# Two of the seven products of a large block as three passes over 12-bit parts

## The chip, the cores and the metric

The kernel runs on one core of a Trainium2 chip. The metric is the device time of one execution in microseconds (us), lower is better. The core has a matrix engine (TensorE, PE in the profile, with PEld for its weight loads), a vector engine (VectorE, DVE), a scalar engine (ScalarE, ACT), a general engine (GpSimd, POOL), and a queue that issues DMA transfers (SyncE, SP). Each engine carries out its own instructions strictly in order; semaphores make one wait for another. All data here are float32.

## The reference

A retention recurrence over 4 batches, 8 heads, 768 positions and 64 channels gives 3072 tokens of 512 channels; behind it stands a two-layer network with an ELU. What is computed:

```python
state = gamma[None, :, None, None] * state + np.einsum('bhd,bhe->bhde', k[:, :, t], v[:, :, t])
y[:, :, t] = scale * np.einsum('bhd,bhde->bhe', q[:, :, t], state)
...
x = attn_out.transpose(0, 2, 1, 3).reshape(B * S, H * D)
h = x @ w_in                                          # (3072, 512) @ (512, 2048)
g = np.where(h > 0.0, h, np.exp(np.minimum(h, 0.0)) - 1.0)
return (g @ w_out).astype(np.float32)                 # (3072, 2048) @ (2048, 512)
```

## The kernel before

The retention runs in chunks of 128 positions; four chunks make a block of 512 tokens, six blocks in all. Its steps (`retention_step`, `scores`, `states`) are spread among the matrix products of the network. `load` fetches a chunk (1024 KB), `scale_v` (L293) multiplies its values, on GpSimd mostly.

Both products of the network use the Strassen-Winograd scheme: a product of matrices cut in 2x2 quarters is made of seven products M1 to M7 of sums of quarters in place of eight. In this kernel's numbering the sums of the first GEMM's result are

- C11 = M1+M2
- C21 = M1+M6+M7+M4
- C22 = M1+M6+M7+M5
- C12 = M1+M6+M5+M3

Block 0 has a plain first GEMM. Block 1 uses the scheme once, in four columns n = 0 to 3 (`first(n)`, L732, and `strassen`, L730 and before it). In a column the products P1, P2, P6, P7, P5, P3, P4 follow each other on TensorE at 1.73 us each, and between them the loop over n (L1567 on) interleaves the end of the column before, the decoding of weights, sums of weights for later blocks, and retention steps. The column's copies (`kept`, L714) lift a product off PSUM on ScalarE; P6 of a column continues on the bank that P1 used, so it waits for that copy.

Blocks 2 and 3, and 4 and 5, form two large blocks of 1024 tokens (nb = 0 and 1). Their first GEMM uses the scheme with large quarters. M2, M3, M1 and M7 are themselves computed by an inner Strassen-Winograd, `big_twice`, in eight steps `at` = 0 to 7 (two per product). The results are kept in SBUF: M2 and M3 in the places of C11 and C12, M7 in that of C22, M1 in a tile of its own. Beside these steps VectorE works off `xparts`, the sums of inputs that the products need; `big_layer_x` makes those of M7, M5, M6 and M4. Then M6, M4 and M5 follow as plain products, in a loop over eight tiles n of 128 rows by 512 columns (L1676 to L1815 and `big_rest`, L1194). A large weight slice of 256 KB per product and pair of tiles is kept in a ring of slots; `want` names the slices in order, `done` gives a slot back and issues the next fetch on SP.

In that loop, per tile: a seed copies M1 into a PSUM bank (L1657), M6 is added there by two matmuls, a second seed (L1661) copies this sum to a second bank, M4 is added there and M5 to the first. VectorE adds M7, or M7 and M3, or the sum for C12, from SBUF (`big_sum`, L1211). The ELU of each result is begun on ScalarE by a Relu and an Exp (`big_elu`, L1217 and L1218, three buffers r) and ended on VectorE (L1219). The engine orders are those in which the program issues: the schedule is made by hand.

After the loop `second_big` (L1236 on) makes the second GEMM of the large block, again with an inner scheme; its products (L1251), copies `ms` (L1259) and sums run over 128x256 tiles. Its first input sums (L1233 and L897) lie at the end of the loop. SBUF is cut into pools: `mpool` holds lifted products and results, `stage` and `t4` serve the early part, and the ring `wq` and the input sums `ts` use their space later. PSUM has banks a (2), b, d, f, and four shared ones (`ps_r`).

Lines of the code before that the steps touch: L293 (`scale_v`), L501 and L502 (ELU of block 1), L714, L719 (copies and sums of `strassen`), L768 (its products), L1155, L1166 and L1170 (products, lifts and sums of `big_twice`), L1202, L1211, L1217 to L1219, L1233, L1251, L1259.

Of the kernel before, what the change touches and what calls it, by code (L numbers as in the profile page):

```python
# [10 lines left out]
FP32 = mybir.dt.float32  # L11
I32 = mybir.dt.int32
# [3 lines left out]
ALU = mybir.AluOpType  # L16


@with_exitstack
def kernel(  # L20
# [7 lines left out]
    scratch4: bass.AP,  # L28
    out: bass.AP,
# [55 lines left out]

    early = ctx.enter_context(ExitStack())
    stage = early.enter_context(tc.tile_pool(name="stage", bufs=3, side="right"))
    t4 = early.enter_context(tc.tile_pool(name="t4", bufs=1, side="right"))
# [792 lines left out]
    PLANE = {6: 0, 5: 1, 4: 2}  # L881

    def send_layer(j, ns):

        for n in ns:
            to_send.append((
                scratch4[PLANE[j], n].rearrange("p (f c) -> p f c", f=2), LAYER[j][:, n].rearrange("p f k c -> p f (k c)")
            ))

    xs = {}  # L890
# [176 lines left out]
    ts_slots = []  # L1067

    def next_ts():
        ts_slots.append(ts_slots.pop(0))  # L1070
        return ts_slots[-1]
# [4 lines left out]
    def want_first(n):  # L1076
# [7 lines left out]
        def layer(j, m):  # L1084
            if n:
                want((tb, "r", j, m), scratch4[PLANE[j], m])

# [11 lines left out]
        for m in range(NQ):  # L1099
            layer(6, m)  # L1100
            if m == 0:
                piece(*before, 3)
            layer(4, m)
            layer(5, m)
# [3 lines left out]
    def big_x(j):  # L1108

        x, t, first_k = xb2 if j == 3 else xa, next_ts(), 0 if j == 1 else 2  # L1110
        yield from inner_x(j, t, *(x[:, first_k + k, TH * u : TH * u + TH] for k in range(2) for u in range(2)))
# [9 lines left out]
    def big_layer_x():  # L1121

        sub = lambda o, x, y: nc.vector.tensor_tensor(out=o, in0=x, in1=y, op=ALU.subtract)
        b11, b12, b21, b22 = (
            x[:, 2 * r : 2 * r + 2].rearrange("p k (h t) -> p k h t", h=2) for r in range(2) for x in (xa, xb2)
        )
        t3 = next_ts()
        sub(t3, b22, b12)
        yield
        t1, t2, t7, t4_ = (next_ts() for _ in range(4))  # L1130
        yield from inner_x(7, t7, *(t3[:, a, b] for a in range(2) for b in range(2)))
        layer_x.update({5: t1, 6: t2, 4: t4_})
        sub(t1, b12, b11)
        yield
        sub(t2, b22, t1)
        yield
        sub(t4_, b21, t2)
        yield

    PLACE = {1: "M1", 2: "C11", 3: "C12", 7: "C22"}  # L1140

    def big_twice(n, j, at):
# [20 lines left out]
        def lift(ps, o=None):  # L1163
            if o is None:
                o = mpool.tile([P, 2, TH], FP32, name="m", tag="m")
            nc.scalar.copy(o, ps)  # L1166
            return o
# [26 lines left out]
    def big_rest(n, m, j, ps):  # L1194

        name = (n + 2, "r", j, m // 2)
        if n:
            w = where[name].rearrange("p (f k d) -> p f k d", f=2, k=2)[:, m % 2]
        else:
            w = LAYER[j][:, m // 2, m % 2]  # L1200
        for k in range(2):
            nc.tensor.matmul(  # L1202
                ps, lhsT=w[:, k, :], rhs=layer_x[j][:, k], start=False, stop=(k == 1),
                skip_group_check=True,
# [4 lines left out]
    def big_sum(x, m, ps):  # L1209

        nc.vector.tensor_tensor(out=tile_of(x, m), in0=ps, in1=tile_of("C22" if x == "C21" else x, m), op=ALU.add)  # L1211

    def big_elu(x, m):

        g = tile_of(x, m)
        r = epool.tile([P, 512], FP32, name="r", tag="r", bufs=3).rearrange("p (t c) -> p t c", t=2)
        nc.scalar.activation(r, g, AF.Relu, scale=-1.0)  # L1217
        nc.scalar.activation(r, r, AF.Exp, scale=-1.0)  # L1218
        return lambda: nc.vector.scalar_tensor_tensor(g, r, -1.0, g, ALU.add, ALU.max)  # L1219
# [16 lines left out]
    def second_big(nb, behind_last):  # L1236
# [3 lines left out]
        def input_parts(j):  # L1240
            x = INPUT2[j]
            t = [next_ts() for _ in range(4)]
# [24 lines left out]
        def inner(j):  # L1267
            res = mpool.tile([P, 2, 2, TH], FP32, name="res", tag="m")
# [297 lines left out]
    some(smalls[2], 1)  # L1566
    for n in range(NQ):  # L1567
        if n < 3:
            load(2 * CPB + n)
# [26 lines left out]
        if n in (1, 2):  # L1596
            run(smalls[n + 1])
        send_small()
    retention_step(2, 1)

    early.close()
    ring_ = ctx.enter_context(tc.tile_pool(name="ring", bufs=1, side="right")).tile([P, 8, 512], FP32, name="wq")
# [291 lines left out]
```

## Time and profile before

| | us |
|---|---|
| median of 3 runs (lowest, highest) | 620.64 (619.3, 620.83) |
| profiled execution, its own time | 620.36 |
| span of that execution in the trace | 618.6 |
| loop over the tiles, nb=0 | 293.99 to 336.12 |
| loop over the tiles, nb=1 | 487.62 to 529.75 |
| TensorE busy in 293.90 to 336.10 | 42.20 of 42.20 |
| VectorE, ScalarE busy in that stretch | 36.64, 37.41 |
| mean granted TensorE clock | 1.00 |

The span is the time from the first to the last instruction in the trace; the run's own time is 1.76 us longer. A group of the profile names a line, an engine, an operation, the tile written and the tiles read, how often it ran, the time that it kept its engine busy, the mean time of one in ns, and the idle time before it with the instruction or transfer that ended most of it. An instruction that reads `x2` in a timeline stands for a run of two equal ones. A float32 matmul leaves two records in the trace.

### The profile page before, as it was taken

The page shows a single profiled execution, that of the slowest core. Times are in us where ns is not written, and L with a number is a line of the kernel's source. Part 1 is how long each engine was busy: PE and PEld are TensorE (multiplying, and loading weights), DVE is VectorE, ACT ScalarE, POOL GpSimd, SP SyncE. Part 2 cuts the span into 40 slices and gives each one's busy share as a digit, 9 for nine tenths or more (in the row PEclk, how much of TensorE's full clock was granted, in tenths as well). Part 3 has the DMA queues.
Part 4 walks back from the last instruction along what each step waited for, and adds up shares of the span by engine and source line. Part 5 has one row for each costly group of instructions (what it writes and reads, how often), then busy time and mean ns, then how long its engine had stood idle before and what let it go on. Part 6 is the DMA issues. An engine that isn't in the chain of part 4 may idle for free.

```text
span 618.6 us, 13412 instructions
## 1 busy us (share of the span) xinstructions
PE 610.7 (99%) x5446; PEld 481.2 (78%) x5446; DVE 494.7 (80%) x777; ACT 261.0 (42%) x446; POOL 22.1 (4%) x29
## 2 busy tenths in 40 slices
PE   8999999999999999999999999999999999999997
PEld 6764568888889998888445888888888644788886
DVE  5769889989889776776988987898446888888785
ACT  5889735105542112236887210010244798511110
POOL 2011000000000010000100000110000000000000
PEclk9999999999999999999999999999999999999999
DMA  8698579789575897786902445874555423456552
GB/s 299 283 385 304 181 216 268 214 251 285 186 233 174 307 375 287 261 262 173 310 1 84 123 133 153 284 260 132 187 159 147 134 69 102 118 152 183 154 154 108
DMA packets 79277, 125.13 MB, mean 202 GB/s; under 512 B 6128, under 2 KB 46832, under 8 KB 74480
## 3 DMA queue, kind: packets, MB, share of 16 engines
q1 hardware_dynamic: 79216, 124.28, 62.4%
q8 instruction: 43, 0.70, 0.5%
q14 instruction: 18, 0.15, 0.1%
HBM read 94.63 MB, written 29.62 MB: 201 GB/s over the span
## 4 chain that ended last, share of the span: by engine, by line
PE 89%; DMA 5%; DVE 3%; ACT 1%; SPq 1%; issue 1%; DVEq 0%
PE pa L1251 15%; PE pa L1155 9%; PE pd L1251 8%; PE pa L1202 6%; PE pd L1155 4%; PE pd L1202 4%; PE pb L1251 4%; PE pa L545 3%; PE x L635 3%; DMA wq<-scratch_dram 3%; PE pa L768 3%; PE pa L927 3%; PE pb L1155 2%; PE pa L635 2%; PE pb L1202 2%; PE y L415 2%
## 5 line engine op out<-in xcount | busy, mean ns | idle before, releaser
L1259 ACT COPY ms<-pa 128x256 f32<-128x256 f32 x41 | 15.3, 372 | 108.6 <-PE pa L1251 105.5
L1251 PE MATMUL pa<-gC,wq 128*128 128x256 f32 x224 | 53.1, 381 | 0.0
L1251 PEld LDWEIGHTS pa<-gC,wq 128*128 128x128 f32 x224 | 42.2, 190 | 6.8 <-DVE gT L1219 0.5
L1218 ACT ACTIVATE r<-r 128x512 f32<-128x512 f32 x64 | 40.3, 630 | 2.0
L1166 ACT COPY m<-pa 128x512 f32<-128x512 f32 x32 | 18.7, 585 | 47.4 <-PE pa L1155 47.4
L293 POOL TENSOR_TENSOR chunk<-chunk,vf 128x512 f32<-128x512 f32 x15 | 19.0, 1265 | 377.2 <-DMA chunk<-in_qkv_dram 201.2
L1263 DVE TENSOR_TENSOR res<-pd,ms 128x256 f32<-128x256 f32 x26 | 10.9, 421 | 25.0 <-PE pd L1251 14.2
L1155 PE MATMUL pa<-ts,wq 128*128 128x256 f32 x104 | 26.9, 384 | 0.0
L1251 PE MATMUL pa<-ts,wq 128*128 128x256 f32 x112 | 26.8, 382 | 0.0
L1251 PE MATMUL pd<-w_all,wq 128*128 128x256 f32 x112 | 26.6, 380 | 0.1
L171 ACT ACTIVATE w_all<-wraw 128x1024 uint32<-128x1024 uint32 (+1 forms) x19 | 19.1, 1007 | 14.7 <-PE x L635 9.8
L1251 PE MATMUL pd<-ts,wq 128*128 128x256 f32 x104 | 24.7, 380 | 0.1
L1233 DVE TENSOR_TENSOR gC<-w_all,gC 128x1024 f32<-128x1024 f32 x20 | 24.2, 1259 | 0.0
L1251 PEld LDWEIGHTS pd<-w_all,wq 128*128 128x128 f32 x112 | 21.2, 190 | 3.4 <-DVE w_all L897 0.5
L1251 PEld LDWEIGHTS pa<-ts,wq 128*128 128x128 f32 x112 | 21.0, 190 | 2.9
L173 ACT ACTIVATE w_all<-wraw 128x1024 fp8e4<-128x1024 f32 (+1 forms) x19 | 22.6, 1192 | 0.6
L1251 PE MATMUL pa<-w_all,wq 128*128 128x256 f32 x96 | 22.9, 381 | 0.0
L1155 PEld LDWEIGHTS pa<-ts,wq 128*128 128x128 f32 x104 | 19.3, 190 | 4.4 <-ACT m L1166 0.7
L1219 DVE SCALAR_TENSOR_TENSOR w_all<-r,w_all 128x512 f32<-128x512 f32 x32 | 21.9, 684 | 0.7 <-ACT r L1218 0.5
L1251 PEld LDWEIGHTS pd<-ts,wq 128*128 128x128 f32 x104 | 19.7, 190 | 3.2 <-DVE ts L897 0.5
L1202 PE MATMUL pa<-ts,wq 128*128 128x512 f32 x48 | 22.1, 592 | 0.0
L1202 PE MATMUL pa<-gC,w_all 128*128 128x512 f32 x48 | 22.1, 592 | 0.0
(327 smaller groups left out, 1456.7 us busy)
## 6 DMA issues: line engine op xcount, KB each, us to landing
wq<-scratch_dram SPq DMA_DIRECT2D x191, 256.0 KB, 3.3
chunk<-in_qkv_dram SPq DMA_DIRECT2D x22, 1024.0 KB, 7.3
wraw<-in_w_dram SPq DMA_DIRECT2D x15, 1024.0 KB, 6.6
out_dram<-res SPq DMA_DIRECT2D x7, 512.0 KB, 2.9
scratch_dram<-gT SPq DMA_DIRECT2D x12, 256.0 KB, 4.3
wq<-scratch_dram SPq DMA_DIRECT2D x24, 128.0 KB, 2.9
scratch_dram<-w_all SPq DMA_DIRECT2D x12, 256.0 KB, 3.9
scratch_dram<-w_all SPq DMA_DIRECT2D x24, 128.0 KB, 2.8
```

What stands on the lines that cost most here:

```text
L171: nc.scalar.activation(flat, lo, AF.Copy, scale=2.0**-29)
L173: nc.scalar.activation(top, hi.bitcast(FP32), AF.Copy, scale=2.0**-120, saturate=False)
L293: eng.tensor_tensor(out=v, in0=v, in1=vf[:, i].unsqueeze(2).to_broadcast([C, H, D]), op=ALU.mult)
L545: nc.tensor.matmul(hp, lhsT=w[n][:, fi, j // 2, j % 2, :], rhs=xb[:, j, :], start=(j == 0), stop=(j == 3))
L635: nc.tensor.matmul(X[j][:, d, :], lhsT=w[j][:, d * P : d * P + P], rhs=x[j], start=(n == 0 and d == 0), stop=at_end, skip_group_check=True,)
L1155: nc.tensor.matmul(ps[:, f, :], lhsT=w[:, f, :], rhs=big_xs[j][k], start=(begin and f == 0), stop=True, skip_group_check=True,)
L1166: nc.scalar.copy(o, ps)
L1202: nc.tensor.matmul(ps, lhsT=w[:, k, :], rhs=layer_x[j][:, k], start=False, stop=(k == 1), skip_group_check=True,)
L1218: nc.scalar.activation(r, r, AF.Exp, scale=-1.0)
L1219: return lambda: nc.vector.scalar_tensor_tensor(g, r, -1.0, g, ALU.add, ALU.max)
L1233: nc.vector.tensor_tensor(out=quarter(to, r, t), in0=quarter(x, r, t), in1=quarter(y, r, t), op=op)
L1251: nc.tensor.matmul(ps, lhsT=w[:, f, :], rhs=ts[j][k][:, f // 2, f % 2, :], start=(begin and f == 0), stop=(f == 3), skip_group_check=True,)
```

## The change

M6 and M4 of the large blocks are computed with operands cut into parts of 12 bits, a weight w = hi + lo (scaled by 2^-12 in one part) and an input x likewise. The parts are kept as float32r, a matmul type of the same 4 bytes. Each of M6 and M4 is the sum of three products of parts: two passes into a PSUM bank, a VectorE operation (`six_sum`, `four_sum`) that multiplies the bank by 4097 and adds a sum from SBUF, and a third pass with the difference of the parts. M5 stays a float32 product.

- `parts_of_layer(n)` cuts the weights of M6 and M4 in block 1's first GEMM, for columns 0 (ahead of n=1), 1 (end of n=1), 2 (start of n=2) and 3 (end of n=2): two ScalarE, two VectorE and two GpSimd operations of 128x512, and two sends of 768 KB to a new scratch in DRAM. Its tile, "wide", has one buffer. All weights of M6 and M4 are fetched back in 24 slices of 256 KB for each large block; before, nb=0 used them in SBUF and nb=1 fetched 12 slices for three products.
- `split_x` cuts the inputs of M6 and M4 in steps 5 to 7 of the inner products, with one operation each of 128x1024 on ScalarE, GpSimd and VectorE.
- `seeds` forms M3-M7 in C12's place and M1+M7 in C22's place on GpSimd, 16 operations of 128x512 for each large block. The seed copies into PSUM and their twins are gone.
- The sum for M4 is not taken from a second bank: `u3` is a ScalarE copy of the finished M1+M6+M7. M5 is added on M6's bank, which then is C22; C12 is formed from that bank by VectorE (`c12_sum`). The ELUs of C21 and C22 read PSUM.
- In the loop the ends of C22 come two tiles later, those of C12 four; after the loop, what is left of them stands beside the first products of `second_big`.
- Chunks for the next blocks are loaded in steps 5 and 6 and at tiles 2 and 5, and scaled after the loop. The tiles for lifted products fall from 5 to 3, with pools of their own in places.

```diff
+    def stt(o, a, by, b, op):
+        nc.vector.scalar_tensor_tensor(o, a, by, b, ALU.mult, op)
+    def parts_of_layer(n):
+        t = wide.tile([P, 2, 6, TH], F32R, name="wp", tag="wp")
+        for at, j in ((0, 6), (2, 4)):
+            w = LAYER[j][:, n].rearrange("p f k d -> p f (k d)")
+            hi, lo, d = (t[:, :, x] for x in (at, at + 1, 4 + at // 2))
+            nc.scalar.activation(hi, w, AF.Copy, scale=R * CUT)
+            stt(lo, hi, -4096.0, w, ALU.add)
+            nc.gpsimd.tensor_tensor(out=d, in0=lo, in1=hi, op=ALU.subtract)
+        for f in range(2):
+            to_send.append((
+                scratch5[2 * n + f].rearrange("q p c -> p q c"),
+                t[:, f].rearrange("p (q h) c -> p q (h c)", h=2).bitcast(FP32),
+            ))
...
+    def split_x(hi, lo, d, x):
+        yield nc.scalar.activation(hi, x, AF.Copy, scale=CUT)
+        yield nc.gpsimd.tensor_tensor(out=lo, in0=x, in1=hi, op=ALU.subtract)
+        yield stt(d, lo, -4096.0, hi, ALU.add)
...
     def big_layer_x():
         sub = lambda o, x, y: nc.vector.tensor_tensor(out=o, in0=x, in1=y, op=ALU.subtract)
...
+        b11, b12, b21, b22 = (x[:, 2 * r : 2 * r + 2] for r in range(2) for x in (xa, xb2))
+        t3 = slots_e[3]
+        sub(t3.rearrange("p k h t -> p k (h t)"), b22, b12)
+        yield
+        sub(b12, b12, b11)
+        layer_x[5] = b12
+        yield
+        sub(b22, b22, b12)
+        planes.update(open_planes())
+        first_split = split_x(*planes[6], b22)
+        next(first_split)
+        next(first_split)
+        yield
+        yield from inner_x(7, slots_e[0], *(t3[:, a, b] for a in range(2) for b in range(2)))
+        next(first_split)
+        yield
+        sub(b21, b21, b22)
+        second_split = split_x(*planes[4], b21)
+        next(second_split)
+        next(second_split)
+        yield
+        next(second_split)
+        yield
...
+    def passes(n, m, j, third, ps):
+        name = (n + 2, "C" if third else {6: "A", 4: "B"}[j], m)
+        todo = [(planes[j][2], 0 if j == 6 else 256)] if third else [(planes[j][0], 0), (planes[j][1], 256)]
+        for x, at in todo:
+            for k in range(2):
+                c = at + k * P
+                nc.tensor.matmul(
+                    joined(ps), lhsT=where[name][:, c : c + P].bitcast(F32R), rhs=x[:, k],
+                    start=(not third and c == 0), stop=(k == 1), skip_group_check=True,
+                )
+        if not third or j == 4:
+            done(name)
...
         g = tile_of(x, m)
+        h = g if h is None else h
         r = epool.tile([P, 512], FP32, name="r", tag="r", bufs=3).rearrange("p (t c) -> p t c", t=2)
-        nc.scalar.activation(r, g, AF.Relu, scale=-1.0)
+        nc.scalar.activation(r, h, AF.Relu, scale=-1.0)
         nc.scalar.activation(r, r, AF.Exp, scale=-1.0)
-        return lambda: nc.vector.scalar_tensor_tensor(g, r, -1.0, g, ALU.add, ALU.max)
+        return lambda: nc.vector.scalar_tensor_tensor(g, r, -1.0, h, ALU.add, ALU.max)
...
     for n in range(NQ):
+        if n == 1:
+            sums_of.close()
+            wide = wide_of.enter_context(tc.tile_pool(name="wide", bufs=1, side="right", reuse_waits="tile"))
+            parts_of_layer(0)
+            send_small()
+        elif n == 2:
+            parts_of_layer(2)
+            send_small()
...
             run(smalls[n + 1])
+            parts_of_layer(2 * n - 1)
         send_small()
...
-        def rest(m, j):
-            big_rest(nb, m, j, qd[m] if j == 4 else qa[m])
-        def seed(m):
-            qa[m] = bank("aab"[m % 3])
-            nc.scalar.copy(qa[m], tile_of("M1", m))
-        def second_seed(m):
-            qd[m] = bank("d")
-            (nc.vector.tensor_copy if m in (1, 3, 5) else nc.scalar.copy)(qd[m], qa[m])
-        def sum_(x, m):
-            big_sum(x, m, qd[m] if x == "C21" else qa[m])
+        any_bank = lambda: ps_r.tile([P, 2, TH], FP32, name="x", tag="r")
+        def six(m):
+            q6[m] = any_bank() if m % 4 == 3 else bank("aba"[m % 4])
+            passes(nb, m, 6, False, q6[m])
+        def six_sum(m):
+            stt(q6[m], q6[m], 4097.0, tile_of("C22", m), ALU.add)
+        def four(m):
+            q4[m] = any_bank() if m % 2 else bank("d")
+            passes(nb, m, 4, False, q4[m])
+        def four_sum(m):
+            stt(q4[m], q4[m], 4097.0, u3.pop(m), ALU.add)
+        def c12_sum(m):
+            nc.vector.tensor_tensor(out=tile_of("C12", m), in0=q6[m], in1=tile_of("C12", m), op=ALU.add)
+        def seeds(*ms):
+            for m in ms:
+                x, y, z = tile_of("C12", m), tile_of("C22", m), tile_of("M1", m)
+                nc.gpsimd.tensor_tensor(out=x, in0=x, in1=y, op=ALU.subtract)
+                nc.gpsimd.tensor_tensor(out=y, in0=z, in1=y, op=ALU.add)
...
             for m in ms:
-                ends[x, m] = big_elu(x, m)
+                h = {"C21": q4, "C22": q6}.get(x)
+                ends[x, m] = big_elu(x, m, h and h[m])
...
             if at == 7:
-                seed(0)
+                seeds(0, 1)
...
-        rest(0, 6)
+        six(0)
         big_c11(0, 1)
-        second_seed(0)
         end("C11", 4)
         run(tail)
-        seed(1)
+        seeds(2, 3, 4, 5, 6, 7)
+        six_sum(0)
         begin("C11", 2)
         end("C11", 5)
         for n in range(2 * NQ):
-            if n == 0:
-                rest(0, 4)
-                sum_("C21", 0)
+            passes(nb, n, 6, True, q6[n])
+            u3[n] = mpool.tile([P, 2, TH], FP32, name="m", tag="m")
+            nc.scalar.copy(u3[n], q6[n])
+            four(n)
+            four_sum(n)
+            if n:
+                end("C21", n - 1)
+            else:
                 big_c11(1, 1)
+                begin("C11", 3)
+                end("C11", 2)
             if n < LAST:
-                rest(n + 1, 6)
-            if n == LAST - 1 and nb == 0:
-                ts_slots[2:2] = [
-                    w_all[:, 2 * k : 2 * k + 2, 3072:3584].rearrange("p n (f t) -> p n f t", f=2) for k in range(2)
-                ]
+                six(n + 1)
             if n:
-                begin("C12", n - 1)
+                big_rest(nb, n - 1, q6[n - 1])
+            if n < LAST:
+                six_sum(n + 1)
+            if n > 1:
+                end("C22", n - 2)
+            if n > 3:
+                end("C12", n - 4)
             late = {1: 6, 3: 7}.get(n)
             if late:
                 end("C11", late)
-            if n + 2 <= LAST:
-                seed(n + 2)
+            if n == 2:
+                begin("C11", 7)
+            elif n > 2:
+                begin("C12", n - 3)
             if n:
+                c12_sum(n - 1)
                 begin("C22", n - 1)
-                end("C21", n - 1)
-                end("C12", n - 1)
-            else:
-                begin("C11", 3)
-                end("C11", 2)
-            if n:
-                rest(n, 4)
-                sum_("C21", n)
-            if n < LAST:
-                second_seed(n + 1)
-            begin("C21", n)
-            if n:
-                end("C22", n - 1)
             else:
                 end("C11", 3)
-            if n in (0, 2):
-                begin("C11", 6 + n // 2)
-            if more and n in (0, 1, 3, 5):
-                bring(groups[0], (n + 1) // 2)
+            passes(nb, n, 4, True, q4[n])
+            begin("C21", n)
+            if n == 0:
+                begin("C11", 6)
+            if more and n in (2, 5):
+                load(groups[0] * CPB + 2 + n // 5)
             if n == LAST:
                 next(sec)
                 next(sec)
-            rest(n, 5)
-            sum_("C12", n)
-            sum_("C22", n)
...
+        big_rest(nb, LAST, q6[LAST])
+        end("C22", LAST - 1)
+        end("C12", LAST - 3)
+        begin("C12", LAST - 2)
...
+        end("C21", LAST)
+        c12_sum(LAST)
...
+        begin("C22", LAST)
         next(sec)
+        end("C12", LAST - 2)
+        begin("C12", LAST - 1)
+        next(sec)
+        end("C22", LAST)
+        end("C12", LAST - 1)
         begin("C12", LAST)
-        next(sec)
-        begin("C22", LAST)
-        end("C21", LAST)
         end("C12", LAST)
-        end("C22", LAST)
+        if more:
+            for n in range(CPB):
+                scale_v(groups[0] * CPB + n)
```

## The prediction

> **What bounds the kernel now.** I read the page's busy shares and its chain of waits first: they say which engine sets the end.
>
> ```profile
> PE 610.7 (99%) x5446; PEld 481.2 (78%) x5446; DVE 494.7 (80%) x777; ACT 261.0 (42%) x446; POOL 22.1 (4%) x29
> ...
> PE 89%; DMA 5%; DVE 3%; ACT 1%; SPq 1%; issue 1%; DVEq 0%
> ```
>
> TensorE works 610.7 of 618.6 us, so work taken off it can shorten the run by as much, if nobody else becomes late. Next the stretches, one for block 1's first GEMM, where the change puts the new parts, and one for the loop over the row tiles of the first large block (columns: stretch, its length, then busy time of PE, PEld, DVE, ACT, POOL, the granted clock, the DMA share, GB/s).
>
> ```profile
> 153.00:162.00 9.00, 9.00 (x44) 7.92 (x43) 8.63 (x14) 4.64 (x8) 0.00 (x0) 1.00 0.94 343
> ...
> 293.90:336.10 42.20, 42.20 (x102) 18.96 (x101) 36.64 (x56) 37.41 (x65) 4.38 (x4) 1.00 0.42 138
> ```
>
> The averages of 80% and 42% mislead: in the loop VectorE is busy 87% and ScalarE 89% beside a TensorE that never stops, and in block 1 the DMA stands at 0.94. Those are the two places to fear. Then the loop's instructions by shape (count | busy us, mean ns of one), and its timeline (start, length):
>
> ```profile
> L1202 PE MATMUL pa<-gC,w_all 128*128 128x512 f32 x48 | 22.1, 592 | 0.0
> L1211 DVE TENSOR_TENSOR w_all<-pd,w_all 128x512 f32<-128x512 f32 x8 | 5.5, 691 | 3.1 <-PE pd L1202 3.1
> L1657 ACT COPY pa<-chunk 128x512 f32<-128x512 f32 x5 | 2.9, 581 | 0.0
> ...
> 296.86 1.29 DVE L1219 SCALAR_TENSOR_TENSOR gC<-r,gC 128x512 f32<-128x512 f32 x2
> 298.55 0.69 DVE L1211 TENSOR_TENSOR w_all<-pd,w_all 128x512 f32<-128x512 f32 x1 [0.41 <-PE pd L1202]
> 299.62 0.62 ACT L1217 ACTIVATE r<-gC 128x512 f32<-128x512 f32 x1
> 300.27 0.63 ACT L1218 ACTIVATE r<-r 128x512 f32<-128x512 f32 x1
> 300.81 0.61 ACT L1217 ACTIVATE r<-w_all 128x512 f32<-128x512 f32 x1
> ```
>
> So: a float32 product of 128x512 is two records; 49 products fill 42.1 us, 0.86 us each, 0.43 a record. VectorE issues 128x512 operations 0.60 apart when queued (two in 1.29), ScalarE a Relu-Exp pair every 1.19 (299.62 to 300.81: 0.65 and 0.54), a copy takes 0.58.
>
> **The change, part by part.** The sum is made against the profiled execution: span 618.6, time 620.36, which lies 0.28 under the median 620.64.
>
> *Passes.* Per row tile M6 and M4 fall from 2 products each (1.72 us) to 6 one-pass matmuls each. No row shows float32r. A float32 record of 0.43 covers two passes if a product has four, so one pass would be 0.215; the bounds are 0.215 and the whole product's 0.86. I take 0.215: 6x0.215 = 1.29, a gain of 0.43 on 16 products in two blocks: 32x0.43 = 13.7 us of TensorE. A row tile falls from 5.15 to 4.30 us. At 0.43 a pass it would be 6.9. The fetches of 24x256 KB a block (3.3 us each in the row below) land under a stage of over 35 us: nothing, at most 2 if queued behind a store.
>
> ```profile
> wq<-scratch_dram SPq DMA_DIRECT2D x191, 256.0 KB, 3.3
> chunk<-in_qkv_dram SPq DMA_DIRECT2D x22, 1024.0 KB, 7.3
> ```
>
> *Early parts.* parts_of_layer(1) stands at the end of column n=1, parts_of_layer(2) at the start of n=2, and both write one tile ("wide", one buffer) from which 2x768 KB are sent. So the first ScalarE instruction of the second waits for the sends of the first. In the old timeline ScalarE gets free of C22's ELU at 158.2. Counted from there: two copies of 0.58 to 159.4, two VectorE operations behind work it has to 161.5, two GpSimd subtractions to 163.0, the send issued then. 1.57 MB at the 350 GB/s of these stretches is 4.5, a landing lag of 1.4 as an estimate (256 KB take 3.3 from issue, of which 0.75 is transfer at that rate): 169.3. Behind the waiting instruction in ScalarE's queue is m1, the copy that product P6 of n=2 needs. Two copies and m1 bring that to 171.05, where the old trace has P6 at 161.50; TensorE has nothing else. Price +9.5 (bounds 6 with sends at 400 GB/s and parts ready 1.5 sooner, 12 with DMA shared by the loads of 1024 KB running there). parts_of_layer(3) at n=2's end delays VectorE sums for P7 of n=3: +1.4 (0 to 3).
>
> The granted clock is 1.00 in every slice before, yet the first two 128x512 records of the run take 2.08 us together, where two take 1.02 in the loop (0.43 and 0.59): TensorE starts slow after rest, and no later idle of this trace is long enough to tell. [...] I leave it out of the sum.
>
> *Before the loop.* The splits put a ScalarE instruction that waits for a VectorE subtraction into the queue ahead of a lift: at step 5 of the inner products 0.7 us. At steps 6 and 7 the second split's hi waits for the subtraction into b21 and holds the lift m1 of step 7 from 288.1 to 291.5, so its P6 slips by 1.9. VectorE's d of that split then waits for GpSimd's lo (128x1024, twice the width of the row's 1.04 us below: about 2), with sums for TensorE behind it. Both go into the start of the loop below. The 16 GpSimd seeds a block are 128x512 with two SBUF inputs. Their row:
>
> ```profile
> 395.29 1.82 POOL L293 TENSOR_TENSOR chunk<-chunk,vf 128x512 f32<-128x512 f32 x1 [63.91 <-DMA chunk<-in_qkv_dram]
> ...
> 396.12 2.07 DVE L1233 TENSOR_TENSOR gT<-w_all,gC 128x1024 f32<-128x1024 f32 x1
> ...
> 398.45 1.04 POOL L293 TENSOR_TENSOR chunk<-chunk,vf 128x512 f32<-128x512 f32 x1 [1.34 <-DMA chunk<-in_qkv_dram]
> ```
>
> 1.04 alone, 1.82 beside a VectorE sum of two SBUF tiles, which itself takes 2.07 instead of 1.22. Seeds start near 295 and the second, which six_sum(0) needs, ends near 299.5: six_sum(0) ends at 300.6 and the third pass of M6, tile 0 runs at 300.7. With nothing late it would run at 295.7.
>
> *The loop's cycle.* From tile 3 on the queues close a ring. VectorE: four_sum(n), C21's end, six_sum(n+1), C22's end, C12's end, c12_sum: five spacings of 0.60 and a last 0.68 = 3.68. The Relu of C22 then waits for c12_sum, which reads the same bank. ScalarE: Relu and Exp of C22, of C21 (0.61+0.54 each, from PSUM), then the copy u3 for the next tile, 0.58 = 2.88. four_sum of the next tile waits for u3. With 0.1 of handovers one turn is 6.65 us, against TensorE's 4.30 and the 5.15 of before. The first tiles turn faster, since C12's and C22's ends are not there yet: counted through the queues, the third passes of tiles 1 to 7 start at 306.7, 311.05, 316.45, 322.55, 329.2, 335.85, 342.5. Tile 7's u3 is at 347.15, its last pass at 348.35, M5 ends at 350.1. Before, the stage ended at 336.1: +14.0 a block with the entry. Had the ring no grip, the block would gain 6.9: the step from -6.9 to +14.0 is what I bet on. TensorE's own 35.3 us of work lie wholly inside.
>
> *The exit.* After the loop ScalarE has B22 of tile 7, which waits for c12_sum(7); that stands on VectorE behind three or four 1.22-us input sums and three ends, to about 357.4. Behind B22 waits the copy of second_big's first product, which its P6 needs: P6 at 359.0, where TensorE is ready at 353.55: +5.5 a block (bounds 2 and 8, by one or three input sums more or fewer in between). Removed seed copies, C21's and C22's sums and 2 MB of stores cost ScalarE and VectorE nothing here: they were hidden by TensorE.
>
> Sum: 620.4 + 9.5 + 1.4 + 2x(0.7 + 14.0 + 5.5) = 671.7. I say 671.
>
> **The rivals.** *TensorE stays the bound* (faster). The place is the loop: if ScalarE and VectorE keep step with 4.30 us a tile, the 13.7 us come through, and waits before and after are hidden: 620.4 - 13.7 = 606.7. For it: 99% busy, and VectorE has slack of 13% there, with fewer sums afterwards. Against: the ring's 6.65 is made of durations that stand in rows, and an order of queues cannot be overtaken. It decides from the point at which ring and entry cost under 6.9 a block and the early wait under 1.
>
> *The ring is loose, the waits stay.* If Relu of C22 does not wait for c12_sum, VectorE's 3.7 and ScalarE's 4.0 (two pairs, C12's pair, a copy) run beside each other, a tile takes 4.3 to 4.9, and the early wait and some of entry and exit are left: 620.4 - 13.7 + 9.5 + 2x(2 to 6) = 620 to 628, up to 640 with entry and exit whole. For: the two read the same bank, and only the order of waiting makes one follow the other. Against: the wait stands in the changed program.
>
> *A pass is no quarter.* That the three passes are no less work than the product they replace: at 0.43 a pass TensorE needs 6.9 a tile, near the ring: +2 to 5 on the forecast, 674 to 677. At 0.86, as a full product, 12.0 a tile: 8x5.35x2 = 86 more, 757. For it only that no row shows the type. Against: two records a product.
>
> **How the numbers follow.** The forecast's own terms give 671 with 645 to 690 by their bounds (early 6 to 12, exit 2 to 8, loop 8 to 17 a block): chance 0.72. The loose ring, 620 to 640: 0.12. TensorE's bound, 607: 0.12. Long passes: 0.04. The range from 624 to 690 holds the forecast and most of the loose ring, 0.8 in all. A change of 0.3%, 1.9 us, is about what a measurement here can tell from none. Faster is the second rival's 0.12; the same 0.02, out of the loose ring's lower end; slower 0.86.
>
> **What would show it.** Right: a TensorE gap of about 9.5 us near 161, with the first instruction of parts_of_layer released by a DMA; matmul records of 0.215 in passes; third passes 6.6 us apart from tile 3, the Relu of C22 released by VectorE's c12_sum and four_sum by ScalarE's u3; the copy ms late after the loop. Wrong: no gap at 161 (the sends landed early), tiles 4.3 apart with TensorE busy, C22's Relu starting with M5's end, seeds of 1 us each, or records of 0.43.

## The result

| | us |
|---|---|
| before, median of 4 runs | 620.32 (619.3 to 620.83) |
| changed, median of 4 runs | 690.7 (690.13 to 692.66) |
| ratio, 95% interval | 1.114 (1.1116 to 1.1169) |
| span of the profiled execution, before and changed | 618.6, 688.9 |

Slower by 70 us, where 51 were forecast: the time lies 0.7 us above the range. The page of the changed kernel, its busy shares, its slices of TensorE and of the granted clock (the share of its full clock that TensorE was given), and its chain of waits:

```profile
PE 629.8 (91%) x5510; PEld 502.9 (73%) x5510; DVE 514.7 (75%) x783; ACT 263.4 (38%) x448; POOL 91.9 (13%) x73
...
PE   8999999994999999995977899999999597699998
...
PEclk9999999998799999997999999999999799889999
...
PE 71%; DVE 14%; ACT 7%; issue 3%; DMA 3%; POOL 1%; SPq 0%; DVEq 0%; ACTq 0%
```

Before, TensorE was 89% of the chain and no slice of the clock was under 9. Now the two engines of the loop's queues make up 21%, and in the four slices where TensorE's busy share is at 6 tenths or less (4, 5, 5 and 6), the clock is at 8, 7, 7 and 8. TensorE's busy time has grown by 19.1 us (610.7 to 629.8) though it has less to do: the same work takes longer where the granted clock is 0.50 (eight records of L780 take 3.78 us at 172.20, and 1.89 at 161.43). Who TensorE waited for (line, tile, releaser: total, times, longest):

```profile
PE pa L1287 <- DVE pa L902: 9.7, 6, 4.0
PE pa L780 <- ACT m L726: 8.9, 1, 8.9
PE pa L1333 <- ACT ms L1341: 8.5, 2, 5.1
PE x L1287 <- DVE x L902: 6.8, 9, 2.3
```

Over all banks the waits of the passes (L1287) for L902 come to 28.1 us. These are the places that the prediction names: L726 is the copy m1 behind the second cut, L902 the sums six_sum and four_sum, L1341 the copy ms after the loop. ScalarE's second cut waited as forecast, for the sends of the first:

```profile
170.53 1.15 ACT L910 ACTIVATE wp<-w_all 128x512 fp32r<-128x512 f32 x2 [9.56 <-DMA scratch_dram<-wp]
```

The windows around them (length, busy time of PE, PEld, DVE, ACT, POOL, granted clock, DMA share, GB/s) show the granted clock, which is 0.50 from 173 to 177. The expectations below call its fall after an idle time the closing of the clock gate:

```profile
161.00:173.00 12.00, 3.12 (x13) 2.42 (x12) 3.26 (x6) 1.62 (x3) 3.90 (x3) 0.74 0.50 183
173.00:177.00 4.00, 2.98 (x7) 1.78 (x6) 4.00 (x6) 2.38 (x4) 2.29 (x2) 0.50 0.20 74
177.00:192.00 15.00, 14.86 (x178) 12.66 (x179) 11.37 (x20) 7.59 (x13) 2.90 (x2) 0.89 0.99 340
316.00:324.00 8.00, 5.38 (x12) 3.80 (x12) 5.97 (x6) 3.04 (x6) 7.84 (x6) 0.57 0.36 111
324.00:334.00 10.00, 7.29 (x21) 5.20 (x22) 8.00 (x9) 3.05 (x6) 9.77 (x7) 0.83 0.34 106
```

Matching TensorE's instructions of the two traces one by one shows where the lag grows (in us, start after less start before):

| stretch | forecast | lag grows by |
|---|---|---|
| block 1's first GEMM | 10.9 | 15.7: 1.5 at P7 of n=1, 9.2 at P6 of n=2, 5.0 in the products behind it (1.1 of it a wait for a VectorE sum) |
| nb=0, steps 5 to 7 | 0.7 + 1.9 | 0.4 + 1.7 |
| nb=0, the loop without these 1.9 | 12.1 | 20.0 |
| nb=0, exit | 5.5 | 5.4 |
| nb=1, all of it | 20.2 | 27.5: 2.2 in the steps, 17.9 in the loop, 7.3 at the exit |
| sum (the spans differ by 70.3) | 51.3 | 70.7 |

### The profile page after: what moved, and what is told of

The parts are those of the page before. It is cut to its first block, busy times and chain, and to the rows that moved or that the text cites. A ratio compares the mean times of both kernels' runs of the same rounds, so it can differ in the third digit from the quotient of the medians.

```text
span 688.9 us, 13713 instructions
## 1 busy us (share of the span) xinstructions
PE 629.8 (91%) x5510; PEld 502.9 (73%) x5510; DVE 514.7 (75%) x783; ACT 263.4 (38%) x448; POOL 91.9 (13%) x73
## 4 chain that ended last, share of the span: by engine, by line
PE 71%; DVE 14%; ACT 7%; issue 3%; DMA 3%; POOL 1%; SPq 0%; DVEq 0%; ACTq 0%
PE pa L1333 15%; PE pa L1225 7%; PE pd L1333 7%; PE pa L960 4%; PE pb L1333 4%; PE pd L1225 3%; PE pa L557 3%; PE x L647 3%; ACT r L1300 3%; ACT r L1299 2%; DVE gC L1301 2%; DMA chunk<-in_qkv_dram 2%; DVE w_all L1301 2%; PE pa L647 2%; PE pd L960 2%
## 5 line engine op out<-in xcount | busy, mean ns | idle before, releaser
L1333 PE MATMUL pa<-gC,wq 128*128 128x256 f32 x240 | 60.8, 401 | 8.5 <-ACT ms L1341 8.5
L1333 PEld LDWEIGHTS pa<-gC,wq 128*128 128x128 f32 x240 | 47.4, 200 | 17.9 <-ACT ms L1341 9.3
L1341 ACT COPY ms<-pa 128x256 f32<-128x256 f32 x41 | 15.3, 372 | 111.6 <-PE pa L1333 105.5
L912 POOL TENSOR_TENSOR wp<-wp 128x512 fp32r<-128x512 f32 x8 | 12.4, 1564 | 124.6 <-DVE wp L902 124.6
L1287 PE MATMUL pa<-xr,wq 128*128 128x512 f32 x48 | 17.9, 491 | 9.7 <-DVE pa L902 9.7
L1301 DVE SCALAR_TENSOR_TENSOR gC<-r,gC 128x512 f32<-128x512 f32 x24 | 26.0, 1082 | 0.0
L780 PE MATMUL pa<-xb,w_all 128*128 128x256 f32 x64 | 17.1, 414 | 8.9 <-ACT m L726 8.9
L1768 POOL TENSOR_TENSOR w_all<-chunk,w_all 128x512 f32<-128x512 f32 x16 | 24.5, 1529 | 1.3
L183 ACT ACTIVATE w_all<-wraw 128x1024 uint32<-128x1024 uint32 (+1 forms) x19 | 19.1, 1006 | 13.8 <-PE x L647 10.0
L1333 PE MATMUL pa<-ts,wq 128*128 128x256 f32 x96 | 22.9, 381 | 0.0
L902 DVE SCALAR_TENSOR_TENSOR pd<-pd,m 128x512 f32<-128x512 f32 x8 | 5.6, 700 | 21.8 <-ACT m L1877 17.7
L780 PEld LDWEIGHTS pa<-xb,w_all 128*128 128x128 f32 x64 | 13.1, 208 | 11.5 <-ACT m L726 9.5
```

Source lines behind the costliest of these rows:

```text
L183: nc.scalar.activation(flat, lo, AF.Copy, scale=2.0**-29)
L780: nc.tensor.matmul(ps[:, fi, :], lhsT=w[:, fi, j2, :], rhs=x[:, j2, :], start=(begin and fi == 0 and j2 == 0), stop=(j2 == 1), skip_group_ ...
L1301: return lambda: nc.vector.scalar_tensor_tensor(g, r, -1.0, h, ALU.add, ALU.max)
L1333: nc.tensor.matmul(ps, lhsT=w[:, f, :], rhs=ts[j][k][:, f // 2, f % 2, :], start=(begin and f == 0), stop=(f == 3), skip_group_check=True,)
L1768: nc.gpsimd.tensor_tensor(out=y, in0=z, in1=y, op=ALU.add)
```

## The experiments

Unless said otherwise, each starts from the changed kernel (690.7), and its time is the median of four runs beside the kernel before.

**The early cut, moved.** The parts of columns 2 and 3 are cut at the end of their own column.

```diff
-        elif n == 2:
-            parts_of_layer(2)
-            send_small()
...
-            parts_of_layer(2 * n - 1)
+        if n:
+            parts_of_layer(n)
```

> The parts of column 2 are cut at the end of column n=2 and those of column 3 at the end of n=3, so that no two cuts stand back to back; nothing else moves. The page of the changed kernel has one 8.9 us idle of TensorE before P6 of n=2, and the granted clock is 0.5 for 13.65 us from 166.7, in which TensorE works 7.0 us. Theory (wait and clock gate): both go, 8.9 + 3.5 to 4.1 less, and P6 of n=2 stands within 2 us of its old place: about 677 to 678. Rival A (the wait alone costs, the clock rows mean nothing): 8.9 less, about 682. Rival B (the wait only moves to the next cut, at the end of n=2 or at the first fetches): under 3 us less.

Measured 699.0, 8.3 us more. Two lines of its waits, of TensorE:

```profile
PE pa L960 <- DMA wq<-scratch_dram: 12.2, 1, 12.2
PE pd L780 <- DVE h L731: 3.2, 2, 2.0
```

The wait for m1 is gone, P6 of n=2 starts at 162.05 in place of 172.20, and at the end of the columns the lead is 10.9 us (not the 12.0 that the next expectation takes over). But SyncE's queue holds the first weight fetch behind the last sends: 12.2 us of waiting and 2.2 behind it, where twice eight records (L960) take 2.08 and 1.91 us in place of 1.16 and 1.06 in the kernel before, turn the lead into a lag of 3.5, which is rival B. (The trace is of the fastest of the four runs, 694.5; the rest of the 8.3 it doesn't show.) A second try kept the fetch free of the sends.

```diff
-        elif n == 2:
-            parts_of_layer(2)
-            send_small()
...
-            parts_of_layer(2 * n - 1)
+            parts_of_layer(n)
...
+    with tc.tile_pool(name="wide", bufs=1, side="right", reuse_waits="tile") as wide:
+        parts_of_layer(3)
+        send_small()
```

> Column 2's parts are cut at the end of n=2, column 3's only after block 1's second GEMM, with a tile of their own. In the run with both cuts late, no cut waited for a send, and the columns ran 12.0 us earlier, but SyncE's queue then held the first weight fetch behind the last sends, for 12.2 us. Theory: here that wait goes, and the gain of 12 to 15 us stays: 675.5 to 679. Rival (the DMA traffic itself is what costs, wherever it is put): another wait for a fetch of over 5 us, 684 or more.

Measured 697.7. The lead at the columns' end is 7.0 us, since a chunk of the retention landed late (3.3 us, and 1.6 in the products behind it). Then the new place costs two waits of 5.6 and 4.6 us: ScalarE's cut waits for the space of results that are still being sent (6.23 us, until out_dram<-res lands), and a later lift for the space of the parts (8.86, until scratch_dram<-wp does). The time is the rival's, though neither wait is for a fetch. This is a matter of memory as much as of bandwidth, and the run does not part the two.

**The clock.** TensorE works through the early wait on products that nobody reads.

```diff
+        if fill:
+            fill()
         product(6, pa, False)
...
+            for _ in range(20):
+                nc.tensor.matmul(
+                    x[:, 0, :], lhsT=a11[:, 0, 0, :], rhs=b11[:, 0, :], start=True, stop=True, skip_group_check=True,
+                )
...
+        return strassen(product, use, n == 0, fill if n == 2 else None)
```

> The wait stays; 20 float32 products of 128x256 (10 at 0.86 us of TensorE) whose result nobody reads are put ahead of P6 of n=2, so that TensorE works through the wait. Theory (the idle closes the clock gate): no stretch of granted clock 0.5 near 167 to 180, P6 of n=2 at the same place as in the changed kernel (172.2) or up to 0.5 later, what follows runs at 1.73 us a product at once, total 3 to 4 us less: about 687. Rival (clock rows without effect, the slow products after the wait come from something else, such as the DMA): same time, 690 to 691, products after the wait still 3.5 us.

Measured 694.3, 3.6 more: the expected time failed, but what was expected of P6 held. TensorE's timeline of the changed kernel, and of this one:

```profile
172.20 3.78 PE L780 MATMUL pa<-xb,w_all 128*128 128x256 f32 x8 [8.88 <-ACT m L726]
```

```profile
162.23 8.80 PE L801 MATMUL x<-xt,w_all 128*128 128x256 f32 x40
171.29 2.00 PE L782 MATMUL pa<-xb,w_all 128*128 128x256 f32 x8 [0.26 <-ACT m L726]
176.18 2.62 PE L782 MATMUL pd<-xb,w_all 128*128 128x256 f32 x8 [2.90 <-DVE h L731]
```

The same eight records take 2.00 in place of 3.78, and nothing but the filling was changed: the half clock came there with the idle time, not with the DMA. In the changed kernel the granted clock is 0.50 from 166.67 to 180.32, and the tenth and eleventh slices of its page read 8 and 7; here both read 9. The 1.8 us won are lost again before 188: P7 waits 2.9 us for a sum of VectorE (1.1 before), behind that wait twice eight records take 2.62 and 2.99 us (at 176.18 and 178.60) in place of 1.89, and at 187.9 TensorE waits 1.3 for a chunk. Later slips of about 1 us each (217, 234, 420) have nothing to do with the filling that the trace shows; they stay unexplained. So most of what half clock costs behind the early wait lies before another bound. All large idle times filled:

```diff
...
+            if j == 1:
+                x = ps_r.tile([P, 2, TH], FP32, name="x", tag="r")
+                for _ in range(7 if nb == 0 else 11):
+                    nc.tensor.matmul(
+                        x[:, 0, :], lhsT=ts[1][1][:, 0, 0, 0:P], rhs=ts[1][1][:, 0, 0, :], start=True, stop=True,
+                        skip_group_check=True,
+                    )
             product(j, 6, pa, False)
...
+            if n < 2:
+                fill((17, 11)[n], any_bank())
             passes(nb, n, 6, True, q6[n])
```

> The changed kernel with products that nobody reads put into the longest idle times of TensorE: 19 of 128x256 float32 (8.2 us) ahead of P6 of n=2, 17 and 11 float32r passes (3.8 and 2.5 us) ahead of the third passes of tiles 0 and 1, and 7 or 11 of 128x256 (3.0, 4.7 us) ahead of the first P6 of second_big. Each is a little shorter than the wait that it fills, so no wait is taken away. Theory (the idle closes the clock gate, which then costs by itself): the granted clock rises from 0.960 to over 0.985, and 6 to 13 us go: 678 to 685. Rival (half clock lies where something else binds anyway): clock rises, time stays at 689 to 692.

Measured 685.0 (ratio to before 1.1042, 1.1024 to 1.1061), clock 0.989: 5.7 us less for 93 added matmuls, just inside the time expected. In the trace, which is of the fastest of the four runs and 8.9 us shorter than that of the changed kernel, the gains lie at the start of both loops (2.6 and 2.1 us) and behind both exits (1.7 and 1.8), and none is left of the early one.

**The ring.** C22's ELU is issued ahead of the sum that shares its bank.

```diff
-                c12_sum(n - 1)
                 begin("C22", n - 1)
+                c12_sum(n - 1)
```

> In the loop over the tiles C22's Relu and Exp are issued ahead of c12_sum, and nothing else changes. Theory (ring of queues): ScalarE need not wait for VectorE's sixth operation, the turn falls from 6.63 us to the larger of TensorE's 4.3 and ScalarE's 4.1, 4.3 to 4.8 us; over tiles 3 to 7 that is 4.5 x 1.9 to 2.3 = 8 to 10 us a block, 16 to 20 in all, and some more from a warm clock: 668 to 675. Rival (VectorE or ScalarE is full, whatever the order): turn stays above 6 us, 685 to 691.

Measured 677.1, 13.6 less. One turn of the changed kernel's timeline shows what was untied:

```profile
355.59 0.57 ACT L1877 COPY m<-pb 128x512 f32<-128x512 f32 x1
356.19 0.70 DVE L902 SCALAR_TENSOR_TENSOR x<-x,m 128x512 f32<-128x512 f32 x1 [2.95 <-ACT m L1877]
...
359.19 0.68 DVE L1762 TENSOR_TENSOR gT<-pa,gT 128x512 f32<-128x512 f32 x1
...
359.90 0.60 ACT L1299 ACTIVATE r<-pa 128x512 f32<-128x512 f32 x1 [1.04 <-DVE gT L1762]
...
362.22 0.57 ACT L1877 COPY m<-pa 128x512 f32<-128x512 f32 x1
362.82 0.70 DVE L902 SCALAR_TENSOR_TENSOR pd<-pd,m 128x512 f32<-128x512 f32 x1 [2.95 <-ACT m L1877]
```

VectorE is idle 2.95 us until u3 (L1877), then has its six operations, and only then ScalarE starts the four that stand ahead of the next u3. The start of the copies u3 for tiles 0 to 7 in the traces gives the turn (nb=0, us from one to the next):

| kernel | tiles 0-1 | 1-2 | 2-3 | 3-4 | 4-5 | 5-6 | 6-7 |
|---|---|---|---|---|---|---|---|
| changed | 7.87 | 8.63 | 6.03 | 6.63 | 6.63 | 6.63 | 6.88 |
| C22 ahead of c12_sum | 7.73 | 7.39 | 4.48 | 5.49 | 5.49 | 5.49 | 5.49 |
| and C21's end ahead of four_sum | 8.16 | 6.87 | 4.49 | 5.02 | 5.02 | 5.02 | 5.01 |
| all orders (below) | 8.51 | 4.07 | 4.88 | 4.63 | 4.36 | 4.50 | 4.48 |

5.49 and not 4.3: the total fell 2 us short of the range. A second ring was left, which the timeline of this run names:

```profile
349.67 0.57 ACT L1877 COPY m<-pb 128x512 f32<-128x512 f32 x1
...
350.88 0.68 DVE L1301 SCALAR_TENSOR_TENSOR w_all<-r,pd 128x512 f32<-128x512 f32 x1
...
351.64 0.63 ACT L1299 ACTIVATE r<-gC 128x512 f32<-128x512 f32 x1 [1.41 <-DVE w_all L1301]
```

C12's Relu waits for one of the three buffers r, which C21's end (350.88) sets free.

```diff
-            four_sum(n)
             if n:
                 end("C21", n - 1)
-            else:
+            four_sum(n)
+            if n == 0:
                 big_c11(1, 1)
...
             if n:
+                begin("C22", n - 1)
                 c12_sum(n - 1)
-                begin("C22", n - 1)
```

> C22's ELU ahead of c12_sum, as in the run before, and C21's end ahead of four_sum on VectorE, so that its buffer r comes free while ScalarE makes u3. That run left a turn of 5.49 us, in which ScalarE sits idle 1.41 us before C12's Relu, released by C21's end. Theory (ring): the turn falls by that 1.41 to ScalarE's own 4.1 or TensorE's 4.3, 4.3 to 4.6 us; 1.0 x 4 to 5 tiles x 2 = 8 to 11 us under the 677.1 of that run: 666 to 669. Rival (a third queue takes over, VectorE first): turn over 5.2, 674 to 677.

Measured 673.0, 4.2 under the run before it, with a turn of 5.02: half of what was expected. Shorter waits for r stay (0.28 and 0.56 us a turn). In the trace, of the slowest of the four runs (676.4), a late chunk cost 3.3 us at 188.

**The entry.** Two sums are issued ahead of C11's.

```diff
-        big_c11(0, 1)
-        end("C11", 4)
         run(tail)
         seeds(2, 3, 4, 5, 6, 7)
         six_sum(0)
+        big_c11(0, 1)
+        end("C11", 4)
...
-            else:
-                big_c11(1, 1)
-                begin("C11", 3)
-                end("C11", 2)
...
                 six_sum(n + 1)
+            if n == 0:
+                big_c11(1, 1)
+                begin("C11", 3)
+                end("C11", 2)
```

> six_sum(0) and six_sum(1) are issued on VectorE ahead of C11's sums and ends (L1305, L1301), which come right after them. Theory (order of VectorE's queue): third passes of tiles 0 and 1 at 314.8 and about 320.5 in place of 318.54 and 326.71; half of that is lost again to the sums put off; 2 x (3 to 5), and 1 to 4 us of half clock: 675 to 683. Rival (GpSimd sets the pace: its 16 seeds hold VectorE's operations with two SBUF inputs wherever these stand): third pass of tile 3 within 1.5 us of its old 338.9, 687 to 691.

Measured 684.4, 6.3 less, which is 1.4 short of the range. The third pass of tile 0 comes 2.7 us sooner and that of tile 1 4.3; some 3 are left at tile 3 and at the loop's end, so the rival (within 1.5 us) is out. What the sums stood behind, on VectorE and GpSimd of the changed kernel, and TensorE's third pass of tile 0:

```profile
312.30 1.60 POOL L1768 TENSOR_TENSOR w_all<-chunk,w_all 128x512 f32<-128x512 f32 x1
...
313.89 2.31 DVE L1305 TENSOR_TENSOR gC<-gC,chunk 128x1024 f32<-128x1024 f32 x1
...
315.19 2.14 POOL L1768 TENSOR_TENSOR w_all<-chunk,w_all 128x512 f32<-128x512 f32 x1
...
316.12 1.76 DVE L1301 SCALAR_TENSOR_TENSOR gC<-r,gC 128x512 f32<-128x512 f32 x1
...
317.80 0.69 DVE L902 SCALAR_TENSOR_TENSOR pa<-pa,w_all 128x512 f32<-128x512 f32 x1
...
318.54 1.22 PE L1287 MATMUL pa<-xr,wq 128*128 128x512 f32 x2 [3.99 <-DVE pa L902]
```

L1305 and L1301 read two SBUF tiles and take 2.31 and 1.76 us in place of 1.22 and 0.68; L902 beside them reads PSUM and takes its 0.69. The seed that six_sum(0) reads (312.30) ended at 313.90, 3.9 us before six_sum(0) began.

```diff
-                nc.gpsimd.tensor_tensor(out=x, in0=x, in1=y, op=ALU.subtract)
```

> Left out: the 8 GpSimd subtractions a block that take M7 from M3 in C12's place (C12 then holds M7 twice over what it should). Theory (GpSimd's sums and VectorE's sums with two SBUF inputs exclude each other): VectorE's L1301 and L1305 in the first 20 us of the loop return to 0.68 and 1.22 us but for those beside the 8 that stay, third pass of tile 3 stands 3 to 6 us earlier, both blocks: 678 to 685. Rival (order and clock alone make the entry late): under 2 us less, 688 to 691.

Measured 683.8, 6.9 less in the medians. Its trace is of the slowest of the four runs (689.1; the others took 683.0 to 684.2). There the first L1305 of the loop is back at 1.21 us and TensorE waits 1.8 us ahead of tile 0's third pass in place of 4.0, but the later ones beside the seeds that stay still take 2.12 and 1.75, and the third pass of tile 3 stands 2 to 3 us nearer, once the 3.1 us are taken off that the early part ran late, for a chunk above all. The total lies in the range expected; the 3 to 6 us a block at tile 3 were a little too many.

**The exit.** The first two products of second_big and their copy come ahead of C22's last ELU.

```diff
-        begin("C22", LAST)
         next(sec)
+        begin("C22", LAST)
```

> After the loop the first two products of second_big, with the copy ms between them, are issued ahead of C22's ELU of tile 7, and nothing else changes. Theory: P6 of that product no longer waits for the copy (3.4 us idle in block nb=0, 5.1 in nb=1), and the half clock stretch behind it goes too: 8.5 + 2 to 3.4 less, about 679 to 681. Rival (the wait moves to the next use of the same ELU, or the input sums of VectorE set the end): under 4 us less.

Measured 683.9, 6.8 less, 3 us short of what was expected. The wait for ms fell from 8.5 to 4.4 us over both blocks, not to nothing: C12's ELU of tile 5 still stood ahead of the copy and waited for a buffer r.

**All orders, and with the early cut.** The first of these adds C22's end ahead of four_sum and moves the first products of second_big ahead of C12's ELU too; the second also sends the parts in two steps and cuts them 10.7 us or more apart.

```diff
-            four_sum(n)
+            if n > 1:
+                end("C22", n - 2)
             if n:
                 end("C21", n - 1)
...
+            four_sum(n)
...
         big_rest(nb, LAST, q6[LAST])
+        next(sec)
+        next(sec)
         end("C22", LAST - 1)
```

> Orders alone, nothing else: C22's ELU ahead of c12_sum; C22's and C21's ends ahead of four_sum (their buffers r come free sooner); six_sum(0) and six_sum(1) ahead of C11's sums; the first products of second_big and the copy ms ahead of the last ELUs. Theory (each term stands alone and they add): 17.7 of the ring and C21's end, 4 to 6 more as ScalarE's two waits of 0.28 and 0.56 us a turn go, 6 of six_sum, 7 to 10 of the exit: 651 to 660. Rival (one queue's relief is given back at the next): over 665.

Measured 653.7 (ratio 1.0522, 1.0487 to 1.0558): within what was expected, the terms add. The turn is 4.50, and TensorE's own work per tile is the floor now: twelve passes, 0.231 us from one to the next (the median in this trace), and M5's 1.72 come to 4.49, and in the turn from 344.37 to 348.87 TensorE is busy all the time.

```diff
+        for a, b in ((0, 2), (2, 3)):
+            for f in range(2):
...
+                parts_of_layer(3)
+                send_small()
             if s == "gap":
+                if n in (1, 2):
+                    parts_of_layer(n)
+                    send_small()
                 break
```

> The same orders, and in block 1 the parts are sent in two steps (hi and lo as soon as they stand, the difference later) and cut at the gap of n=1 and n=2 and in the middle of n=3. Theory: cuts are then 11 us apart and need 8, the 8.9 us wait of P6 goes, and the first fetch waits 2 to 4 us behind the last sends: 8 to 11 less than the run with the orders alone. Rival (the sends cost wherever they stand): less than 3 us under it.

Measured 650.4 (ratio 1.0489, 1.0468 to 1.0509), 3.3 less in place of 8 to 11.

```profile
PE pa L961 <- DMA wq<-scratch_dram: 8.1, 2, 7.2
```

The 8.9 us wait of P6 is gone; 7.2 of it are back at the first weight fetch, which stands behind the sends, and the rest of the lead of 9.0 goes behind that, where twice eight records (L961) take 2.08 and 1.91 us in place of 1.16 and 1.06 in the kernel before. So the 3.3 us were not won in block 1: the two traces are level again there, some 15 us behind the kernel before, and part later, in the loops and exits. What would take these 15 us off was not found. Of the orders and places tried, none brings the kernel under its time before.

## Why the prediction was off

The step that failed is the count of the loop's first tiles, "counted through the queues, the third passes of tiles 1 to 7": this term of the sum was too small. Without what the steps before it brought, the loop cost 20.0 us in nb=0 and 17.9 in nb=1, where 12.1 were forecast for each. That is 13.7 of the 19.4 us missed. The direction and the other mechanisms were right: the wait of ScalarE for the sends (forecast 9.5, 9.2 measured), the ring (forecast 6.65 a turn, 6.63 measured), the hi of the second split (1.9, 1.7), the exit of nb=0 (5.5, 5.4). The runs on the ring bear this out: untying one order took 13.6 us off. Four terms were wrong.

- "Third passes of tiles 1 to 7", and that of tile 0 before them. The forecast lets six_sum(0) go when the second seed ends. In the trace that seed ends 3.9 us before six_sum(0) begins, which stands behind C11's sum and end on VectorE, each 1.1 us longer than alone. The seeds and C11's operations slow each other at more places than the one priced (the seeds in nb=0's loop took 1.26 to 2.25 us, where 1.04 was read for one operation alone): third passes of tiles 0 to 3 came 1.8, 3.9, 5.8 and 6.3 us later than worked out (with the lag of 16.1 at the loop's start added), then the lag stayed at 6.2; in nb=1 it was 5.6 at the end. Most of the rest of nb=0's loop, 1.7 us, is tile 7's M5 at half clock (L1274 at 371.02: 3.16 us in place of 1.88, the granted clock 0.50 from 371.46 to 374.88). The order on VectorE, GpSimd's sums and the half clock each have a share in the 6 us; singly their runs took off 6.3, 6.9 and part of the 5.7 us over both blocks, and they overlap, so the shares are not known one by one.
- "I leave it out of the sum", of TensorE's slow start after rest. By the trace's record of the granted clock, TensorE had half clock (0.50) for 55 us in ten stretches and worked 43 us of them, which is 21.6 us of its work lost. Not all of that was on the path: filling the idle times took 5.7 us off the median. Six of the stretches lasted 3.41 us, three 6.83 and one 13.65. In the 3.41 us ahead of each, TensorE was busy 1.83 us or less. When the trace's times at full clock are cut into steps of 3.41 us, the least busy step that another one follows (from 10 us on; 361.23 to 364.64) has 1.93. Inside the stretches, half clock went on after steps with up to 2.49 us of work and ended after steps with 3.18 or more; after the early idle it lasted 13.65 us, of which TensorE worked 7.0. These are the figures of one trace, and what sets them it does not show.
- The parts of column 0 were priced at nothing. They cost 1.5 us: a VectorE sum (L867) took 1.75 us in place of 0.68 beside GpSimd's subtraction, and P7 waited. The 1.4 forecast at P7 of n=3 did not come.
- The exit's 5.5 has the right size for a partly wrong reason: 3.4 us are the wait for ms and 2.0 the half clock behind it (granted 0.50 from 381.70 to 385.12); in nb=1 it was 5.1 and 2.2 (0.50 from 600.16 to 606.99).

Some of the working was off without harm. A pass took 0.231 us from one to the next, not 0.215 (that a float32 product has four passes was the author's assumption), so each of the two products saves 1.72 - 6x0.231 = 0.33 a tile and not 0.43. It did not matter, as the forecast held, while the ring of VectorE and ScalarE set the pace. The early wait's parts add up to 168.9 and not 169.3, and its landing lag of 1.4 doesn't follow from the row beside it (3.3 less 0.75 is 2.55); and GpSimd's two subtractions took 2.9 us where 1.5 were counted, which VectorE, done 0.7 us sooner, and their overlap made up for. So the good size is in part luck. The stated bounds of the terms add up to 648 to 687 and not to 645 to 690: block 1's first GEMM (15.7 against at most 15) and the loop with its 1.9 (21.8 and 19.7 against at most 17) lay beyond theirs. Of the rivals, the loose ring had its turn right (5.49 with C22's ELU alone moved, but 4.50 with all orders changed, in its 4.3 to 4.9) and its total wrong: 653.7 in place of 620 to 640, since more of the early part, the entry and the exit stays. The early wait was sized right, but the view that removing it would give its 9.5 us back was not: in three tries the time went to the next fetch, to the next chunk or to memory in use.

## What to carry to other kernels

Before moving work from a matrix engine that never stops to engines that are 87% and 89% busy in the same stretch, walk each queue for one turn: an engine whose first instruction waits for the other's last makes the turn the sum of both (6.63 us, where 4.50 were possible, and an exchange of two lines gave half of the difference). Price an idle of TensorE above its length: here 55 us ran at a granted clock of 0.50 behind idle or half-idle stretches. A saving of 0.7 us a tile has to pay for every send, cut and seed that makes it possible, and here even with the rings untied it did not.

## What was not expected of the hardware

- Half clock (granted 0.50) came here without a single long idle: a stretch began at 371.5 us after an idle of 2.3 (368.1 to 370.5), and those at 572.9 and 586.5 after 3.41 us with no idle over 1.2, in which TensorE was busy by about half (1.80 and 1.83 us).
- Sums of 128x512 with a PSUM operand kept their 0.69 us beside GpSimd, while those with two SBUF operands went from 0.68 up to 1.78 (L1301 at 331.57), also in the scalar-tensor-tensor form that ends an ELU.
- Filling TensorE's idle times with products that nobody reads was a gain in time here: 93 matmuls more, 5.7 us less.
